# Fused attention and two MLPs: another order of the attention round, casts on ScalarE, and transfers planned by a pipe

## The chip, the cores and the metric

One core of a Trainium2 chip runs the whole program in one launch. The metric is the device time of an execution in microseconds. The kernel before took 1013.02, 1010.97 and 1012.54 us in three runs, median 1012.54. The profiled execution took 1009.88 us.

## The reference

```python
def _attn_ref(q, k, v):                       # q, k, v: 4 x 12 heads x 448 x 64, float32
    S = q.shape[2]
    scores = (1.0 / np.sqrt(q.shape[-1])) * np.matmul(q, k.transpose(0, 1, 3, 2)) - np.log(S)
    return np.matmul(1.0 / (1.0 + np.exp(-scores)), v)
def _moe_ref(x, w_in, w_out):                 # 1792 x 768, 768 x 2048, 2048 x 768; weights float64
    h = x @ w_in
    return np.where(h > 0.0, h, np.exp(np.minimum(h, 0.0)) - 1.0) @ w_out
def _moe2_ref(x, w_in, w_out):
    h = x @ w_in
    return (h - np.tanh(h)) @ w_out
```

The attention output, with its heads side by side, goes through the first MLP and that through the second.

## The kernel before

**Attention.** Two heads make a pair (n = 0 to 23), two pairs a round (m = 0 to 11). A head has 448 keys: three blocks of 128 and a rest of 64. For each pair TensorE transposes q and k (`t`), VectorE or ScalarE copies the result out of PSUM (`plain`), VectorE casts it (`hi`, L335) and takes what the cast lost (`lo`, L339), TensorE makes three blocks of scores (`s`, L358), ScalarE takes their sigmoid (`sig`, L379), and TensorE multiplies by v (`pv`, L387). The keys' rests of both pairs of a round share one product (`sr`, L369), one sigmoid (`sigr`, L375, tile `ar`) and one value product (`pvr`, L397), which closes the sums that `pv` opened. VectorE copies the sums out (`xdone`, L408). Three PSUM buffers go round between `s`, `sr` and every other `t`.

**MLPs.** Each is done by Strassen's seven products with one level of Winograd sums, and each operand is split into a rounded half and a remainder (`head` on ScalarE, `rest` on VectorE), so a product is three matmuls. Tokens are in two halves (s = 0 with 512 columns, s = 1 with 384). T1 to T4 are sums of blocks of attention output (L759), L769 and L775 split them. Products P1, P2, P5, P6, P3, P7, P4 are L803. `snap` (L815) saves a product from PSUM, `h_add` (L820) adds the next.

**Preparation during attention.** Weights come as float64 and are narrowed with integer operations: one step on ScalarE (L598), two on VectorE (L601, L605). All of the first `w_out` (16 loads of 768 KB, L649) is narrowed, summed (L658) and stored again (L663) while attention runs, and four blocks of `w_in` too (L580, L582, tiles R1a, R1b).

**What sets the order.** Nothing is scheduled on the chip: each engine runs its list in order and waits on semaphores. The lists come from a planner (`Sched`). It first places the attention alone by the phases of a round (`PHASES`, in ns), then all of it again; there an operation of the MLPs may take an engine only if the next attention operation of that engine is not put off by more than `GIVE`. All loads and stores are issued by SP's queue (SyncE), in one order too.

Of the kernel before, what the change touches and what calls it, by code (L numbers as in the profile page):

```python
# [9 lines left out]
F32 = mybir.dt.float32  # L10
# [6 lines left out]
class Sched:  # L17
# [3 lines left out]
    def __init__(self):  # L21
        self.ops, self.before, self.plan = {}, {}, {}
# [7 lines left out]

    def emit(self, only_plan=False):
        ops, plan, late = self.ops, self.plan, 0

        planned = {q: sorted((k for k in plan if ops[k][0] == q), key=plan.get, reverse=True) for q in ("ACT", "DVE")}
        after = {k: [a for a in o[3] if a in ops] for k, o in ops.items()}
# [11 lines left out]
        while any(ready.values()):  # L47
            best = None
            for queue, keys in ready.items():
                t0 = free.get(queue, 0)  # L50
                for k, t in keys.items():
                    c = (max(t, t0), ops[k][4], str(k))
                    if k not in plan and planned.get(queue) and c[0] + ops[k][1] > plan[planned[queue][-1]] + late + GIVE:
                        c = (10 ** 9,) + c[1:]
                    if best is None or c < best[0]:
                        best = c, queue, k
            (start, rank, _), queue, k = best
            start = max(ready[queue][k], free.get(queue, 0))
            if k in plan:
                late = start - plan[k]  # L60
# [22 lines left out]
GIVE = 100  # L83

ROUND = 2 * CYCLE
PHASES = {
    "s": ((0, 600, 1200), (3900, 4500, 5100)), "sig": ((1100, 2100, 3100), (5100, 6100, 7100)),
    "pv": ((5900, 6650, 7400), (8150, 8900, 9650)), "pvr": 10500, "xdone": (11400, 12000),
    "sr": -700, "sigr": 50,
    "t": (2000 - ROUND, 2900 - ROUND), "plain": (2950 - ROUND, 4100 - ROUND), "hi": (4100 - ROUND, 5800 - ROUND), "lo": (4700 - ROUND, 6400 - ROUND),  # L90
# [4 lines left out]
SHIFTS = {(0, "ldv"): -12000, (0, "sr"): 2550, (0, "sigr"): 2600, (0, "ldvr"): -11000}  # L95
# [3 lines left out]
def kernel(  # L99
# [67 lines left out]
    with tc.manual_schedule():  # L167
# [7 lines left out]
        def attention():  # L175
# [31 lines left out]
            vrest = [vs_p.tile([128, NR, D], F32, name=f"vrest{i}") for i in range(2)]  # L207
# [20 lines left out]
            def rests(w, g):  # L228
                return heads[w][2 * NR * g:2 * NR * (g + 1), KW:S]

            def ld_kr(g):
                for y in range(NR):
                    i, x = divmod(y, 2)
                    nc.sync.dma_start(
                        out=krest[g % 2][RS * x:RS * x + RS, i].rearrange("p (h d) -> p h d", h=2),
                        in_=rests(0, g)[2 * y:2 * y + 2].rearrange("h p d -> p h d"),
                    )

            def ld_vr(g):
                for z in range(2):  # L240
                    for x in range(2):
                        nc.sync.dma_start(
                            out=vrest[g % 2][RS * z:RS * z + RS].rearrange("p (i x) d -> x p i d", x=2)[x],
                            in_=rests(1, g).rearrange("(i x h) p d -> x h p i d", x=2, h=2)[x, z ^ x],
                        )
# [18 lines left out]
            def when(kind, n, *rest):  # L264
                at = PHASES[kind]
                if kind not in ("sr", "sigr", "pvr", "ldk", "ldv"):
# [6 lines left out]
            def loads(m):  # L273


                g = m * NL // NR
                todo = [("ldv", m, 0, NL)]
                if m * NL % NR == 0:
                    todo = [("ldkr", g)] + todo + [("ldvr", g)]
# [5 lines left out]
                fns = {"ldv": ld_v, "ldkr": ld_kr, "ldvr": ld_vr, "ldkfirst": lambda i: ld_first("k", i), "ldqfirst": lambda i: ld_first("q", i)}  # L285
                for x, key in enumerate(todo):
# [3 lines left out]
                        "ldkr": [("t", NR * (g - 2) + 2)], "ldvr": [("pvr", 2 * (g - 2) + 1)],  # L290
                    }.get(kind, [])
                    sch.op(key, "SP", {"ldkr": 2400, "ldvr": 2400}.get(kind, 600), lambda fn=fns[kind], args=args: fn(*args),
                           after, when("ldv" if kind[2] == "v" else "ldk", m) + x, 2500)

            def loaded(kind, n):
# [4 lines left out]
                return part + ([("ldkr", n // NR)] if n % 2 == 0 else [])  # L300
# [8 lines left out]
            def transpose(n):  # L309
# [5 lines left out]
                for c in range(R):  # L315
                    nc.tensor.transpose(ps[:, DD + KW + c * SP:DD + KW + (c + 1) * SP], ql[:, n % NL, c], ident[:SP, :SP])

            def parts_of(n):
                lo, hi = DD * (n % 2), DD + EW
                return [("ACT", lo, DD + KW), ("DVE", DD + KW, hi)] if n == 0 else [(("DVE", "ACT")[n % 2], lo, hi)]  # L320

            def to_plain(n, x):
# [10 lines left out]

            def hi(n):
                nc.vector.tensor_copy(out=es[n % 2][:, :EW], in_=kq(n))  # L335
# [45 lines left out]
            def pv(n, u):  # L381
                m, x = divmod(n, 2)
                if (x, u) == (0, 0):
                    T["o", m] = pso.tile([128, 2, BK], F32, tag="o", name="pvps")
# [6 lines left out]
            def pv_rest(m):  # L391
                a = T.pop(("a", m))
                for x in range(2):
                    n = 2 * m + x
                    for j in range(2):
                        lanes = slice(64 * (j ^ x), 64 * (j ^ x) + 64)
# [1137 lines left out]
```

## Time and profile before

| | |
|---|---|
| median of three runs | 1012.54 us |
| profiled execution | 1009.88 us, span 1008.2 us |
| PE busy | 977.1 us, 97% |
| DVE, ACT, POOL busy | 780.1, 597.4, 112.1 us |
| granted TensorE clock | 0.988 of full speed, mean |
| HBM traffic | 142.61 MB read, 74.97 MB written |

PE, DVE, ACT and POOL are TensorE, VectorE, ScalarE and GpSimd. Attention takes PE until 171.2 us, the first MLP follows. Since PE is busy nearly everywhere, the places to look at are those where it is not.

### The profile page before, as it was taken

How to read it: one execution, taken by the hardware profiler on the slowest of the kernel's cores; microseconds unless marked ns; L12 is line 12 of the kernel's file. 1: busy time of each engine (PE TensorE's matmuls, PEld its weight loads, DVE VectorE, ACT ScalarE, POOL GpSimd, SP SyncE). 2: the span in 40 equal slices, each digit the busy share in tenths (PEclk: the TensorE clock that was granted, in tenths of full speed). 3: DMA queues.
4: the chain of work that ended last, by engine and by line, in shares of the span. 5: the costliest groups of instructions: out<-in, count | busy, mean ns of one | idle time of the engine just before them, and what ended most of it. 6: DMA issues, size and time to landing. Idle time of an engine off the chain costs nothing.

```text
span 1008.2 us, 15604 instructions
## 1 busy us (share of the span) xinstructions
PE 977.1 (97%) x5306; PEld 844.7 (84%) x5306; DVE 780.1 (77%) x1143; ACT 597.4 (59%) x943; POOL 112.1 (11%) x110
## 2 busy tenths in 40 slices
PE   8989899689999999999999998999999999999998
PEld 5555455578888888888899997888888999999998
DVE  4879798977888888668887899777777788665673
ACT  4768578756666667665566654444444556446652
POOL 2211220202222220000000201111111000000000
PEclk9989899989999999999999999999999999999999
DMA  7899981066666679999984734455555894455442
GB/s 205 286 299 317 300 300 64 31 186 191 191 191 191 191 241 321 372 401 382 373 284 131 242 97 148 160 196 188 186 192 187 325 330 146 125 169 173 128 148 85
DMA packets 145087, 218.61 MB, mean 217 GB/s; under 512 B 21936, under 2 KB 103408, under 8 KB 144752
## 3 DMA queue, kind: packets, MB, share of 16 engines
q1 hardware_dynamic: 143744, 217.10, 64.6%
q8 instruction: 41, 0.67, 0.3%
q10 hardware_dynamic: 1264, 0.52, 0.2%
q14 instruction: 38, 0.31, 0.1%
HBM read 142.61 MB, written 74.97 MB: 216 GB/s over the span
## 4 chain that ended last, share of the span: by engine, by line
PE 90%; DMA 4%; DVE 2%; ACT 1%; issue 1%; SPq 0%; ACTq 0%; DVEq 0%
PE psa L803 13%; PE psd L803 12%; PE psx L803 10%; PE psu L958 7%; PE psv L958 7%; PE psw L958 7%; PE psa L958 6%; PE psb L958 6%; PE psb L803 5%; PE psy L958 5%; PE sps L358 4%; PE pvps L387 4%; PE psx L958 3%; PE psd L958 1%; DMA XB<-in_moe_w_out_dram 1%; DMA vl<-in_v_dram 1%
## 5 line engine op out<-in xcount | busy, mean ns | idle before, releaser
L930 ACT ACTIVATE XB<-t 128x384 fp32r<-128x384 f32 (+1 forms) x111 | 62.0, 562 | 37.5 <-PE psw L958 9.9
L718 POOL TENSOR_TENSOR second<-second 128x384 f32<-128x384 f32 x15 | 19.2, 1279 | 552.1 <-DMA t<-x_forms 213.5
L934 DVE TENSOR_TENSOR XB<-t,XB 128x384 fp32r<-128x384 f32 (+1 forms) x111 | 68.3, 626 | 11.4 <-ACT XB L930 11.1
L379 ACT ACTIVATE an<-sps,bias 128x896 f32<-128x896 f32 x72 | 68.6, 1008 | 3.7 <-PE pvps L387 2.0
L358 PE MATMUL sps<-e 64*128 64x448 f32 x432 | 55.1, 395 | 9.7 <-ACT ar L375 9.3
L358 PEld LDWEIGHTS sps<-e 64*128 64x128 f32 x432 | 40.3, 197 | 25.1 <-ACT ar L375 10.5
L930 ACT ACTIVATE XB<-spare 128x512 fp32r<-128x512 f32 (+1 forms) x72 | 41.1, 573 | 27.0 <-PE psw L958 11.2
L387 PE MATMUL pvps<-an,vl 128*64 128x448 f32 x288 | 56.8, 543 | 0.0
L803 PE MATMUL psa<-XB,W 128*128 128x512 f32 x192 | 54.6, 393 | 0.0
L934 DVE TENSOR_TENSOR XB<-spare,XB 128x512 fp32r<-128x512 f32 (+1 forms) x72 | 44.2, 622 | 8.0 <-ACT XB L930 7.7
L958 PE MATMUL psu<-XB,XB 128*128 128x384 f32 (+1 forms) x192 | 46.3, 348 | 0.0
L226 POOL COPY first<-raw_qk 128x384 f32<-128x384 f32 (+1 forms) x44 | 34.2, 798 | 109.1 <-DMA raw_qk<-in_k_dram 79.5
L958 PE MATMUL psv<-XB,XB 128*128 128x384 f32 (+1 forms) x192 | 46.1, 348 | 0.0
L958 PE MATMUL psw<-XB,XB 128*128 128x384 f32 (+1 forms) x192 | 46.1, 348 | 0.0
L387 PEld LDWEIGHTS pvps<-an,vl 128*64 128x64 f32 x288 | 19.6, 137 | 31.6 <-issue 29.1
L803 PEld LDWEIGHTS psa<-XB,W 128*128 128x128 f32 x192 | 36.4, 190 | 7.7
L832 ACT ACTIVATE spare<-t 128x512 f32<-128x512 f32 (+1 forms) x33 | 19.0, 579 | 36.9 <-DVE t L820 35.9
L718 POOL TENSOR_TENSOR first<-first,second 128x384 f32<-128x384 f32 x30 | 40.1, 1336 | 1.2
L803 PE MATMUL psd<-XB,W 128*128 128x512 f32 x144 | 37.0, 401 | 1.5 <-DVE W L735 1.3
L836 ACT ACTIVATE spare<-spare 128x512 f32<-128x512 f32 (+1 forms) x64 | 36.6, 572 | 0.7
L958 PE MATMUL psa<-XB,XB 128*128 128x384 f32 (+1 forms) x156 | 36.8, 347 | 0.0
L958 PE MATMUL psb<-XB,XB 128*128 128x384 f32 (+1 forms) x156 | 36.8, 347 | 0.0
(362 smaller groups left out, 2732.6 us busy)
## 6 DMA issues: line engine op xcount, KB each, us to landing
x_forms<-R1b SPq DMA_DIRECT2D x58, 256.0 KB, 2.0
first<-p_forms SPq DMA_DIRECT2D x36, 384.0 KB, 6.3
t<-x_forms SPq DMA_DIRECT2D x64, 192.0 KB, 2.9
t<-x_forms SPq DMA_DIRECT2D x47, 256.0 KB, 4.9
x_forms<-t SPq DMA_DIRECT2D x44, 256.0 KB, 2.0
x_forms<-R1b SPq DMA_DIRECT2D x58, 192.0 KB, 4.7
spare<-x_forms SPq DMA_DIRECT2D x36, 256.0 KB, 4.7
x_forms<-t SPq DMA_DIRECT2D x44, 192.0 KB, 3.4
```

The source lines that it names most:

```text
L226: nc.gpsimd.tensor_copy(out=(ql, kl)[w][:, n % NL].rearrange("p c (h d) -> p c h d", h=2), in_=x)
L358: nc.tensor.matmul(out=ps[:, j, :S], lhsT=e[lanes, EW * kz + u * 128:EW * kz + (u + 1) * 128], rhs=e[lanes, EW * qz + KW:EW * qz + EW], st ...
L379: nc.scalar.activation(out=a, in_=T.pop(("s", n, u))[:, :, :S], func=ACTF.Sigmoid, bias=bias, scale=scale)
L387: nc.tensor.matmul(out=T["o", m][D * j:D * j + D, j ^ x, :S], lhsT=vl[m % NVL][:, x, 3 * j + u], rhs=a[:, j], start=(u == 0), stop=False,)
L718: by.tensor_tensor(out=out, in0=x, in1=y, op=op)
L803: nc.tensor.matmul(out=ps, lhsT=w[wz][:, k0:k0 + 128], rhs=xs[xz][:, kk], start=(opens and n == 0), stop=(n == 3 * KH - 1), skip_group_che ...
L832: nc.scalar.activation(out=r, in_=h, func=ACTF.Tanh)
L836: nc.scalar.activation(out=r, in_=r, func=ACTF.Exp, scale=-1.0)
L930: nc.scalar.activation(out=at_place(og_place[i, s, p, j], 0, i)[:, :HW[s]], in_=T["graw", i, s, p, j], func=ACTF.Copy)
L934: nc.vector.tensor_tensor(out=lo, in0=T.pop(("graw", i, s, p, j)), in1=f(hi), op=ALU.subtract)
L958: nc.tensor.matmul(out=T["o2", tag], lhsT=lhsT, rhs=rhs, start=(p in OPENS and j == 0 and x == 0), stop=(j == NG - 1 and x == 2), skip_gro ...
```

## The change

Round: `pvr` now comes ahead of `pv` on TensorE, opens the sums and waits for nothing that `pv` makes; each pair has a PSUM bank of its own, so `xdone` waits for its own pair's `pv` only. The rests lie on other lanes, and the loads of `w_in` need no swapped halves and are one DMA, not three. `hi` of even pairs is on ScalarE. The rests' loads come two DMAs a round instead of four every other round. In the planner a DMA now lands when a pipe shared by all has moved it (`moves`, ns for each kind), `w_out` loads start a round earlier and are paced, an attention operation on ScalarE or VectorE may be put off by 0.6 of its slack, and only TensorE's lateness counts as lateness. The s = 1 operands are made in one piece of 1152 columns, not three of 384, and T3 and T4 of that half are summed on GpSimd. Line numbers after the change are 7 to 27 higher.

```diff
+SLACK = 0.6
+PACE = 7500
-    "s": ((0, 600, 1200), (3900, 4500, 5100)), "sig": ((1100, 2100, 3100), (5100, 6100, 7100)),
-    "pv": ((5900, 6650, 7400), (8150, 8900, 9650)), "pvr": 10500, "xdone": (11400, 12000),
+    "s": ((0, 650, 1250), (3850, 4500, 5100)), "sig": ((700, 1600, 2500), (5200, 6100, 8250)),
+    "pvr": 5800, "pv": ((7400, 8150, 8900), (9650, 10400, 11150)), "xdone": (9750, 12000),
...
+        return {k: plan[k] + SLACK * (t - plan[k]) for k, t in found.items()}
...
-                    if k not in plan and planned.get(queue) and c[0] + ops[k][1] > plan[planned[queue][-1]] + late + GIVE:
+                    if k not in plan and planned.get(queue) and c[0] + ops[k][1] > limit[planned[queue][-1]] + late + GIVE:
...
+            if k in self.moves:
+                moved = max(moved, start + 1400) + self.moves[k]
+                done[k] = moved + 600
...
+            def ld_rests(w, m):
+                g, i = m // 2 % 2, m % 2
+                for x in range(2):
+                    h = 4 * m + 2 * x
+                    to = vrest[g][RS * x:RS * x + RS, i] if w else krest[g][RS * x:RS * x + RS, i].rearrange("p (h d) -> p h d", h=2)
+                    nc.sync.dma_start(out=to, in_=heads[w][h:h + 2, KW:S].rearrange("h p d -> p h d"))
...
+                if hi_on(n) == "ACT":
+                    nc.scalar.activation(out=es[n % 2][:, :EW], in_=kq(n), func=ACTF.Copy)
...
-                        lanes, c = slice(64 * j, 64 * j + 64), 64 * (j ^ x)
+                        lanes, c = slice(64 * j, 64 * j + 64), 64 * x
...
-                        out=T["o", m][D * j:D * j + D, j ^ x, :S], lhsT=vl[m % NVL][:, x, 3 * j + u], rhs=a[:, j], start=(u == 0), stop=False,
+                        out=T["o", m][D * j:D * j + D, x, :S], lhsT=vl[m % NVL][:, x, 3 * j + u], rhs=a[:, j], start=False, stop=(u == 2), skip_group_check=True,
...
-                    op(("pvr", m), "PE", 850, pv_rest, [("sigr", m), ("ldvr", n // NR)] + [("pv", n - y, 2) for y in range(2)])
+                    op(("pvr", m), "PE", 850, pv_rest, [("sigr", m), ("ldvr", m)] + opens)
...
-                        op(("xdone", y), "DVE", 680 if pairs[y][0] == 2 else 630, xdone, [("pvr", m)] + (before if y == 2 * NP else []))
+                        op(("xdone", y), "DVE", 680 if pairs[y][0] == 2 else 630, xdone, [("pv", y, 2)] + (before if y == 2 * NP else []))
...
-                return (slice(None),) if i else range(KH)
+                return (slice(None),) if i or s else range(KH)
...
-                return "DVE"
+                return "POOL" if (i, s) == (0, 1) and x in ("T3", "T4") else "DVE"
...
-                    op("p_load", (j, c), "SP", 600, p_load, [("s", 1, 0)] + (was[c:c + 1] if wide else held), 11000)
+                    sch.moves["p_load", j, c] = 2150
+                    paced = (2 * j + c) * PACE // CYCLE
+                    op("p_load", (j, c), "SP", 600, p_load, ([("s", paced, 0)] if paced else [("t", 1)]) + (was[c:c + 1] if wide else held), 11000)
```

**ScalarE, attention, the fourth and fifth `ar` of the program.** Before, in the round that ends in the first long wait (L598 narrows; R1a is a `w_in` block, XB_71 and XA_70 hold blocks of `w_out`):

```order
L375 ACTIVATE ar<-sps,bias 128x896
L379 ACTIVATE an<-sps,bias 128x896 x3
L327 ACTIVATE plain_122<-sps 128x832
L379 ACTIVATE an<-sps,bias 128x896 x2
L598 ACTIVATE XB_71<-XB_71 128x768
L379 ACTIVATE an<-sps,bias 128x896
L598 ACTIVATE XB_71<-XB_71 128x768
L598 ACTIVATE R1b<-R1a 128x768
L375 ACTIVATE ar<-sps,bias 128x896
```

After, around the narrowing of the same block (L394 is `ar`, L398 `an`, L352 the cast, L605 narrows):

```order
L394 ACTIVATE ar<-sps,bias 128x896
L398 ACTIVATE an<-sps,bias 128x896 x4
L340 ACTIVATE plain_122<-sps 128x832
L352 ACTIVATE e_83<-plain_121 128x832
L398 ACTIVATE an<-sps,bias 128x896
L605 ACTIVATE R1b<-R1a 128x768
L398 ACTIVATE an<-sps,bias 128x896
L394 ACTIVATE ar<-sps,bias 128x896
L398 ACTIVATE an<-sps,bias 128x896
L605 ACTIVATE XB_71<-XB_71 128x768
```

The narrowing has moved from behind the round's last `an` to between two of them.

**SP's queue, the round with most bytes.** Before, from behind one load of `vl` (L259) up to the next, without that first load:

```order
L663 DMA p_forms<-XB_71 128x384
L242 DMA vrest_117<-in_v_dram 64x2x64 x4
L580 DMA R1a<-in_moe_w_in_dram 64x6x256
L582 DMA R1a<-in_moe_w_in_dram 64x3x256 x2
L234 DMA krest_116<-in_k_dram 64x2x64 x4
L663 DMA p_forms<-XB_71 128x2x384
L222 DMA raw_qk<-in_k_dram 128x2x192
L222 DMA raw_qk<-in_q_dram 112x2x256
L222 DMA raw_qk<-in_k_dram 128x2x192
L222 DMA raw_qk<-in_q_dram 112x2x256
L649 DMA XA_70<-in_moe_w_out_dram 128x1536 x2
L663 DMA p_forms<-XB_71 128x4x384
```

After, the fullest round, with its load of `vl` (L274):

```order
L274 DMA vl_119<-in_v_dram 128x4x192
L260 DMA vrest_117<-in_v_dram 64x2x64 x2
L670 DMA p_forms<-XB_71 128x4x384
L656 DMA XB_71<-in_moe_w_out_dram 128x1536
L260 DMA krest_116<-in_k_dram 64x2x64 x2
L249 DMA raw_qk<-in_k_dram 128x2x192
L249 DMA raw_qk<-in_q_dram 112x2x256
L656 DMA XA_70<-in_moe_w_out_dram 128x1536
L249 DMA raw_qk<-in_k_dram 128x2x192
L249 DMA raw_qk<-in_q_dram 112x2x256
L624 DMA kept_wi_2_708<-R1b 128x768
L594 DMA R1a<-in_moe_w_in_dram 128x6x256
```

The big loads now stand apart, and the rests are two DMAs each. A row's bytes are its product times 4.

**VectorE, behind the attention.** Before, from the split of B11 (L775, into R0a) to the sum T3 (the third L759):

```order
L775 TENSOR_TENSOR R0a<-R1a,R0a 128x384 x3
L735 TENSOR_TENSOR R0b<-second,R0a 128x768
L735 TENSOR_TENSOR W_1728<-spare,e_83 128x384
L759 TENSOR_TENSOR R1a<-R1a 128x384 x3
L820 TENSOR_TENSOR t<-t,psb 128x512
L775 TENSOR_TENSOR XB_1805<-R1b,XB_1805 128x384 x3
L820 TENSOR_TENSOR t<-t,psa 128x512
L775 TENSOR_TENSOR R0b<-R1a,R0b 128x384 x3
L759 TENSOR_TENSOR R1a<-R1b,R1a 128x384 x3
L820 TENSOR_TENSOR t<-t,psd 128x512
L846 SCALAR_TENSOR_TENSOR t<-spare,t 128x512
L759 TENSOR_TENSOR R1a<-R1a 128x384 x3
```

After, from the same split (L782) on (L766 is the sum T2, L853 the activation's last step):

```order
L782 TENSOR_TENSOR R0a<-R1a,R0a 128x1152
L782 TENSOR_TENSOR XB_1804<-R1b,XB_1804 128x1152
L742 TENSOR_TENSOR R0b<-second,R0a 128x768
L782 TENSOR_TENSOR R0b<-R1a,R0b 128x1152
L742 TENSOR_TENSOR W_1731<-spare,e_83 128x384
L766 TENSOR_TENSOR R1a<-R1b,R1a 128x3x384
L827 TENSOR_TENSOR t<-t,psb 128x512
L827 TENSOR_TENSOR t<-t,psd 128x512
L827 TENSOR_TENSOR t<-t,psa 128x512
L782 TENSOR_TENSOR XB_1804<-R1a,XB_1804 128x1152
L853 SCALAR_TENSOR_TENSOR t<-spare,t 128x512 x2
L782 TENSOR_TENSOR XB_1804<-R1b,XB_1804 128x1152
```

T1 has gone ahead of the attention's end, T3 and T4 to GpSimd, where they stand behind the last of the attention's copies:

```order
L253 COPY first<-raw_qk 128x384
L253 COPY first<-raw_qk 112x512
L766 TENSOR_TENSOR R1a<-R1a 128x3x384
L766 TENSOR_TENSOR R1b<-R1b,R1a 128x3x384
L725 TENSOR_TENSOR second<-second 128x384
```

GpSimd has nothing else to do in between.

## Rows read from the trace of the kernel before

**Rows 1.** The page: busy time (share of the span) and instructions of each engine.

```profile
PE 977.1 (97%) x5306; PEld 844.7 (84%) x5306; DVE 780.1 (77%) x1143; ACT 597.4 (59%) x943; POOL 112.1 (11%) x110
```

**Rows 2.** Timeline of PE in attention: start, length (us), engine, line, tiles, count, idle.

```profile
61.53 1.49 PE L358 MATMUL sps<-e 64*128 64x448 f32 x12
...
66.90 1.49 PE L358 MATMUL sps<-e 64*128 64x448 f32 x6 [3.89 <-ACT ar L375]
...
111.55 1.49 PE L358 MATMUL sps<-e 64*128 64x448 f32 x6 [4.73 <-ACT ar L375]
...
124.72 0.47 PE L358 MATMUL sps<-e 64*128 64x448 f32 x2
...
160.97 4.76 PE L358 MATMUL sps<-e 64*128 64x448 f32 x36
```

**Rows 3.** Windows: stretch, length, busy us of the engines, granted clock, DMA share, GB/s.

```profile
48.00:60.00 12.00, 12.00 (x95) 6.80 (x94) 11.93 (x15) 9.02 (x10) 4.04 (x6) 1.00 1.05 366
...
61.53:124.72 63.19, 53.84 (x369) 31.31 (x365) 48.46 (x70) 41.09 (x48) 12.69 (x16) 0.89 0.94 302
...
124.72:160.97 36.25, 36.25 (x278) 20.62 (x274) 33.49 (x51) 27.41 (x32) 6.68 (x8) 1.00 0.77 260
...
192.00:204.00 12.00, 3.65 (x18) 3.04 (x18) 12.00 (x25) 8.56 (x18) 0.00 (x0) 0.92 0.17 66
```

**Rows 4.** Waits of PE over the span: total us, times, longest.

```profile
PE sps L358 <- ACT ar L375: 9.3, 3, 4.7
...
PE psd L803 <- ACT R1b L815: 7.2, 1, 7.2
```

**Rows 5.** Timeline of ACT in the two long waits.

```profile
65.06 0.89 ACT L598 ACTIVATE R1b<-R1a 128x768 f32<-128x768 f32 x1 [6.43 <-DMA R1a<-in_moe_w_in_dram]
...
108.68 0.89 ACT L598 ACTIVATE XB<-XA 128x768 f32<-128x768 f32 x1 [1.97 <-DMA XA<-in_moe_w_out_dram]
```

**Rows 6.** DMA issues: form, count, KB each, median us to landing.

```profile
XB<-in_moe_w_out_dram SPq DMA_DIRECT2D x8, 768.0 KB, 8.9
```

**Rows 7.** Timelines behind the attention: PE, DVE and ACT.

```profile
171.23 2.34 PE L803 MATMUL psa<-XA,e 128*128 128x512 f32 x9
...
204.46 1.01 PE L803 MATMUL psd<-XB,R0a 128*128 128x384 f32 x2 [7.21 <-ACT R1b L815]
...
172.44 1.89 DVE L775 TENSOR_TENSOR XB<-R0a,XB 128x512 fp32r<-128x512 f32 x3
...
190.14 2.31 DVE L759 TENSOR_TENSOR R1a<-R1b,R1a 128x384 f32<-128x384 f32 x3
...
203.92 0.49 ACT L815 ACTIVATE R1b<-psd 128x384 f32<-128x384 f32 x1 [2.12 <-DVE R1a L775]
```

**Rows 8.** Groups by shape: line, tiles, shapes, count, busy us, mean ns, idle.

```profile
L327 ACT ACTIVATE plain<-sps 128x832 f32<-128x832 f32 x12 | 10.4, 867 | 6.6 <-PE sps L316 6.6
...
L335 DVE CAST e<-plain 128x832 fp32r<-128x832 f32 x24 | 16.4, 684 | 2.5 <-PE sps L358 1.0 <-ACT plain L327 1.0
...
L775 DVE TENSOR_TENSOR XB<-R0a,XB 128x1536 fp32r<-128x1536 f32 x3 | 5.3, 1756 | 2.0 <-ACT XB L769 2.0
...
L718 POOL TENSOR_TENSOR first<-first,second 128x384 f32<-128x384 f32 x30 | 40.1, 1336 | 1.2
```

**Rows 9.** Timeline of PE, rest products in a clean round.

```profile
159.30 0.98 PE L397 MATMUL pvps<-ar,vrest 64*64 64x448 f32 x8
...
160.11 0.54 PE L369 MATMUL sps<-plain 64*64 64x448 f32 x2
```

**Rows 10.** Timelines of DVE and POOL while POOL adds.

```profile
184.84 1.49 DVE L775 TENSOR_TENSOR XB<-R1b,XB 128x384 fp32r<-128x384 f32 x3
...
186.48 0.69 DVE L820 TENSOR_TENSOR t<-t,psa 128x512 f32<-128x512 f32 x1
...
187.08 3.13 DVE L775 TENSOR_TENSOR R0b<-R1a,R0b 128x384 fp32r<-128x384 f32 x3
...
187.17 1.34 POOL L718 TENSOR_TENSOR first<-first,second 128x384 f32<-128x384 f32 x1
```

More of the change, by code (lines that the diff above doesn't have):

```diff
@@ L21, in __init__ @@
     def __init__(self):
-        self.ops, self.before, self.plan = {}, {}, {}
+        self.ops, self.before, self.plan, self.moves = {}, {}, {}, {}
     def op(self, key, queue, cost, fn, after, rank, latency=60):
@@ L29, in chain, with latest @@
         self.before.update(zip(keys[1:], keys))
+    def latest(self):
+        ops, plan = self.ops, self.plan
+        users, last = {k: [] for k in plan}, {}
+        for k in plan:
+            for a in ops[k][3]:
+                if a in plan:
+                    users[a].append(k)
+        found = {}
+        for k in sorted(plan, key=plan.get, reverse=True):
+            queue, cost, latency = ops[k][0], ops[k][1], ops[k][5]
+            if queue in ("PE", "SP"):
+                found[k] = plan[k]
+            else:
+                by = [found[u] - cost - latency for u in users[k]]
+                if queue in last:
+                    by.append(last[queue] - cost)
+                found[k] = max(plan[k], min(by, default=plan[k]))
+                last[queue] = found[k]
+        return {k: plan[k] + SLACK * (t - plan[k]) for k, t in found.items()}
     def emit(self, only_plan=False):
-        ops, plan, late = self.ops, self.plan, 0
+        ops, plan, late, moved = self.ops, self.plan, 0, 0
         planned = {q: sorted((k for k in plan if ops[k][0] == q), key=plan.get, reverse=True) for q in ("ACT", "DVE")}
+        limit = self.latest() if plan else {}
         after = {k: [a for a in o[3] if a in ops] for k, o in ops.items()}
@@ L59, in emit @@
             if k in plan:
-                late = start - plan[k]
+                late = start - plan[k] if queue == "PE" else late
                 if queue in planned:
@@ L206, in attention @@
             krest = [ld_p.tile([128, 2, DD], F32, name=f"krest{i}") for i in range(2)]
-            vrest = [vs_p.tile([128, NR, D], F32, name=f"vrest{i}") for i in range(2)]
+            vrest = [vs_p.tile([128, NR // 2, 2, D], F32, name=f"vrest{i}") for i in range(2)]
             heads = [x.rearrange("b h s d -> (b h) s d") for x in (k, v)]
@@ L265, in when @@
                 at = PHASES[kind]
-                if kind not in ("sr", "sigr", "pvr", "ldk", "ldv"):
+                if kind not in ("sr", "sigr", "pvr", "ldk", "ldv", "ldqk1"):
                     n, x = divmod(n, 2)
@@ L332, in kq, with hi_on @@
                 return plain[n % 2][:, DD * (1 - n % 2):][:, :EW]
+            def hi_on(n):
+                return "DVE" if n == 0 or n % 2 else "ACT"
             def hi(n):
-                nc.vector.tensor_copy(out=es[n % 2][:, :EW], in_=kq(n))
+                if hi_on(n) == "ACT":
+                    nc.scalar.activation(out=es[n % 2][:, :EW], in_=kq(n), func=ACTF.Copy)
+                else:
+                    nc.vector.tensor_copy(out=es[n % 2][:, :EW], in_=kq(n))
             def lo(n):
@@ L573, in load @@
                     nc.sync.dma_start(out=t[:, :CW], in_=kept[key])
-                elif key[:2] == ("wi", 0):
-                    f0 = key[2] * 128
-                    to = (t.bitcast(I32) if wide else t[:, :CW]).rearrange("p (k f) -> p k f", k=KD)
-                    rows = w_ins[0][:, f0:f0 + 128].bitcast(dt)
-                    nc.sync.dma_start(out=to[:64], in_=rows.rearrange("(k z p) f -> z p k f", z=2, p=64)[0])
-                    for x in range(2):
-                        nc.sync.dma_start(
-                            out=to[64:].rearrange("p (m x) f -> x p m f", x=2)[x],
-                            in_=rows.rearrange("(m x z p) f -> x z p m f", x=2, z=2, p=64)[1 - x, 1],
-                        )
                 elif wide:
@@ L1099, in job @@
                     after.append(("keep", kept_by[key], key))
+                if place == 4:
+                    sch.moves["load", n] = 2700
                 raw_op(("load", n), "SP", 600, lambda: load(n, key, not live), after, 8500 if place == 4 else 8500 if live else 6000)
@@ L1115, in job @@
                     kept_by[key] = n
+                    if place == 4:
+                        fixed["keep", n, key] = n * ROUND + 3
+                    if place == 4:
+                        sch.moves["keep", n, key] = 1100
                     raw_op(("keep", n, key), "SP", 600, lambda: keep(n, key), [done], 12000 if place == 4 else 5600)
@@ L1497, in mlp @@
                 sch.op(k, o[0], o[1], o[2], o[3], fixed.get(k, 10 ** 6 + late_by[k]), o[4])
-            sch.chain([("pvr", NPR // 2 - 1)] + sequence)
+            sch.chain([("pv", NPR - 1, 2)] + sequence)
         attention()
```

75 lines of the change are left out of this document (29 added, 46 removed).

## Prediction

> **What bounds the kernel now.** I read the page first, for how much can be won at all. PE is busy for 977.1 of the 1008.2 us of the span [rows 1], so 31.1 us are idle, and a change that leaves the matmuls alone can win these and what a slow clock adds to them. Then PE's timeline in attention, for where. A round opens with the scores of its even pair. In the clean stretch three rounds take from 124.72 to 160.97, which is 12.08 us each; the four rounds from 61.53 to 124.72 take 63.19 us where four clean ones take 48.33 [rows 2]. So **14.9 us are lost in four rounds of attention**. The windows over the same stretches say what kind of loss it is: PE idles for 9.35 us and has a clock of 0.89 on the mean, where the clean stretch has no idle time and 1.00 [rows 3]. A matmul behind each long wait runs at the lower of the two clocks: 6 of L358 take the 1.49 us that 12 take elsewhere [rows 2]. Nearly all the idle time is one line of the waits, PE's L358 for ACT's `ar` [rows 4], 3.89 and 4.73 us in the two long ones and 0.7 in a third; a long one so costs (14.9 - 0.7) / 2 = 7.1 us with its clock.
>
> ACT is not slow there. It stands in front of a narrowing, L598, whose load has not landed: 6.43 us for R1a at 65.06, 1.97 more for XA at 108.68 [rows 5], and `ar` is queued behind it. The load is late because the DMA engines are full: share 1.05 at 366 GB/s from 48 to 60 us [rows 3]. At that rate a round of 12.08 us moves 4318 KB. Counting SP's order between loads of `vl` (the big ones have 768 KB and land after 8.9 us [rows 6]), the rounds from 51 us on ask for 5120, 4480, 4352, 4480 and 4352 KB, 22784 in all, for which five rounds have room for 21590. No order on ACT could hide that.
>
> The other place lies behind attention. The first product of the MLP starts at 171.23, and before P3 of the second half, at 204.46, PE waits 7.21 us for a snapshot on ACT, which waits for VectorE's last split of T4 [rows 4, 7]. VectorE is busy for all 12.00 us of 192 to 204 [rows 3]. That is the only wait of this size outside attention.
>
> **The change part by part.**
>
> Transfers. After the change the same count gives 4224, 4800, 2688, 4608 and 3840 KB for the five fullest rounds in a row, 20160 in all, under the 21590: the first `w_out` blocks are loaded a round earlier, and the pairs of 768 KB are spread. Two rounds are still over 4318, by 482 and 290 KB, 1.3 and 0.8 us at 366 GB/s. Both are followed by a round with room. So the two long waits go, and I charge 2.1 us for the two overfull rounds as if nothing covered them. Bounds: 0, since 48 to 60 us has a full pipe and no idle PE [rows 3], and 14.9, all of it back. I take 2.1, nearest to the clean row. Term: -14.9 + 2.1.
>
> Casts. Eleven casts leave VectorE (0.68 us each [rows 8]) and go to ACT, which copies as many columns in 0.87 [rows 8]. In attention neither engine sets the end: in the clean stretch ACT is busy for 27.41 of 36.25 us and VectorE for 33.49 [rows 3], and with three casts moved it is 30.0 and 31.4. In the four slow rounds the same preparation fitted into 48.33 us would make ACT 41.09 + 3.5 = 44.6 and VectorE 48.46 - 2.7 = 45.8, 92 and 95%; the order starts it about a round earlier, so some of that moves forward. Cost 0; if the cover is gone (VectorE over 12.08 us in a round) PE waits for the split of q and k, a few tenths a round. What is late next in attention is PE itself.
>
> The rest products. The number of matmuls is the same. The four of `pvr` use the same four quarters of the array in another order; now they take 0.81 us from 159.30 on and the four of `sr` 0.86 to 160.97 [rows 2, 9], so all four overlap, two quarters that share rows and two that share columns among them. Cost 0. If neighbours in the new order did not overlap, both would double, 1.7 us a round and 20 us in all; `sr` already writes two column halves to one bank at once, which speaks against it, and a gain has nothing to come from, since the array is as full. SP's queue: a `w_in` block takes one issue, not three, and a round two plus two rest DMAs instead of runs of eight every other round; its stalls shorten, which is in the term above.
>
> Behind attention. I count VectorE's operations from the first product on (E = 171.23), because PE's wait ends with the last of them. Now it starts its splits at E + 1.2 (172.44), three of 512 columns in 1.89 us, starts the sum T2 at E + 18.9 (190.14), and P3 of the second half starts at E + 33.2 [rows 7]. After: 0.6 for one `xdone` (two took the 1.2), 8 splits of 512 at 0.63 = 5.0, three of 1152 at 1.32 (1.756 us for 1536 [rows 8]) = 4.0, the weights' 768 and 384 = 1.3, T2 itself 1.3: T2 ends at E + 12.2 and no longer at E + 21.2. T1 and two weight sums have gone forward into attention, and one wide instruction has one start-up instead of three.
>
> Then T3 and T4 on GpSimd, 3 x 1.34 = 4.0 us each [rows 8]. Here the trace speaks against the change: while POOL added, three splits of VectorE took 3.13 us instead of 1.49, though an addition of a PSUM operand took its usual 0.69 [rows 10]. Two of the three were held until a GpSimd instruction was over. What follows T2 on VectorE is mostly of the kind that was held: the splits of T2, B22, T3, T4 (1.3 each), three last steps of the activation (0.63 each), one sum (0.6), one weight split (0.9), 8.6 us. T3 holds it to E + 16.2, T4 for 4.0 more, so the last split ends at E + 28.8, the snapshot takes 0.5 [rows 7], and P3 starts at E + 29.3. Gain 33.2 - 29.3 = 3.9 us. Without the holding VectorE is through at E + 12.2 + 1.9 (three additions of products) + 8.6 = E + 22.7, P3 starts at E + 23.2, and the gain is 10.0. I take 3.9, since the held rows are of this very pair of engines. The idle time before P3 is about as long as now, so its slow clock stays.
>
> The Trainium skill states this as a rule, in "SBUF — State Buffer", section "Who interferes with whom": a VectorE instruction with two SBUF inputs and a GpSimd instruction that reads SBUF take one shared port by an exclusive lock for the whole instruction. The trace agrees for instructions of 384 columns; that a 1152-wide one holds VectorE for all of its 4.0 us no run here shows. By the rule the gain is 3.9 us, by a mere sharing of the port nearer to 10.0.
>
> Everything from the second weight group on stays as it is; there PE is busy nearly throughout, and the `w_in` blocks land far ahead.
>
> **Sum** against the profiled execution: 1009.88 - 14.9 + 2.1 - 3.9 = 993.2 us. The median of the runs is 2.66 above that execution, so the time to expect is 995.8.
>
> **The rivals.**
>
> No holding: GpSimd and VectorE share, and nothing is late in the two overfull rounds. 1012.54 - 14.9 - 10.0 = 987.6. For it: in rows 10 every second VectorE instruction still slips in. Against it: the three that took twice as long.
>
> One long wait stays. The narrowings now stand between two sigmoids, close behind their loads, and one load that is late by more than planned repeats the picture of 65.06: 1012.54 - 14.9 + 7.1 - 3.9 = 1000.8, 1003 with the overfull rounds. For it: the two rounds over 4318 KB; against it: the five rounds ask for 1430 KB less than the pipe moves in them, where they now ask for 1194 more.
>
> The waits are only moved: all the same bytes have to go through in attention, and the earlier start changes nothing. Then only the 3.9 us remain: 1008.6. Against it: the clean stretch has a DMA share of 0.77, so there is room to move into.
>
> Slower: ACT's new order makes lateness dear. Before, a narrowing stood behind the round's last `an`, and PE lost 3.89 of ACT's 6.43 us, 2.5 being covered [rows 2, 5]. Now three sigmoids come behind it, and a round's last value product needs them. If loads come over 2.5 us late in several rounds, each costs 7.1 us; from three on (21.3 against the 18.8 won) the kernel is slower, and with four it takes 1022. For it: twenty narrowings are placed this tightly; against it: the bytes a round.
>
> **How the numbers follow.** Forecast 0.47, no holding 0.16, one wait stays 0.20, only moved 0.07, slower by ACT's order 0.10. The range from 985 to 1009 leaves out most of the last case and a little below the second. About 0.2%, 2 us, is what a measurement can tell from no change. Faster by more: the first three and a part of the fourth, 0.85; within it 0.05; slower 0.10.
>
> **What would show it.** Right: round starts 12.1 us apart throughout, PE's wait for `ar` under 2 us in total, a clock of 1.00 until the first product, which starts near 158; full DMA windows with no idle PE; then VectorE splits that take 2 to 4 us beside T3 and T4, and a wait of PE of 6 to 7 us, P3 about 29 us behind the first product. Wrong: PE waiting for `an` or a value product waiting behind a narrowing (the slower rival), rounds over 12.3 us with no wait (rest products that no longer overlap, or VectorE over its round), or a P3 at 23 us.

## The result, and the profile after

The changed kernel takes 998.54 us (median of 4 runs, 998.21 to 999.5) against 1011.75 for the kernel before: ratio 0.9871, 95% interval 0.9854 to 0.9888. On another chip it took 1000.17 against 1008.18, ratio 0.9914 (0.9901 to 0.9927). So it is faster by 0.9 to 1.3%; the forecast of 995.8 was 2.7 us low. Its profiled execution took 998.61 us, with a span of 996.9. The page's busy times, to be read against [rows 1]:

```profile
PE 968.8 (97%) x5306; PEld 837.6 (84%) x5306; DVE 766.8 (77%) x1108; ACT 603.3 (61%) x940; POOL 113.8 (11%) x112
```

The span is 11.3 us shorter, and three places make it up: the first product of the MLP comes 5.66 us sooner, the stretch from there to the second half's P3 is 3.81 us shorter, and the rest 1.8. Those two products in the changed kernel, to be read against [rows 7]:

```profile
165.57 2.34 PE L810 MATMUL psa<-XA,e 128*128 128x512 f32 x9
...
194.99 1.01 PE L810 MATMUL psd<-XB,R0a 128*128 128x384 f32 x2 [7.35 <-ACT R1b L822]
```

PE's waits in attention (us in total, times, longest) answer to [rows 4]:

```profile
PE pvps L404 <- DVE R0a L426: 4.4, 4, 2.0
PE pvps L404 <- DVE R1a L426: 1.8, 2, 0.9
PE pvps L404 <- DVE R1b L426: 1.7, 2, 0.9
PE pvps L404 <- DVE R0b L426: 1.6, 2, 0.8
```

No wait for `ar` is left. In its place stands one that the prediction did not have: a value product (L404) waits for VectorE's copy of the attention output (`xdone`, L426), ten times, 9.5 us. PE's timeline, first a round with that wait and then the start and the end of one without it, to be read against [rows 2]:

```profile
64.48 2.09 PE L377 MATMUL sps<-e 64*128 64x448 f32 x18
...
70.21 0.98 PE L415 MATMUL pvps<-ar,vrest 64*64 64x448 f32 x8
...
71.88 3.23 PE L404 MATMUL pvps<-an,vl 128*64 128x448 f32 x16
75.92 1.72 PE L404 MATMUL pvps<-an,vl 128*64 128x448 f32 x8 [0.82 <-DVE R0a L426]
77.58 0.67 PE L377 MATMUL sps<-e 64*128 64x448 f32 x4
...
130.22 2.08 PE L377 MATMUL sps<-e 64*128 64x448 f32 x18
...
142.26 2.09 PE L377 MATMUL sps<-e 64*128 64x448 f32 x18
```

A round with the wait takes 77.58 - 64.48 = 13.10 us, one without it 142.26 - 130.22 = 12.04. The difference of 1.06 is the wait's 0.82 and some 0.2 more, because the 24 value products take 3.23 + 1.72 us in two parts and 4.73 in one (experiment 1 shows that row). VectorE's side of the same moment shows that it isn't late:

```profile
73.08 0.96 DVE L612 SCALAR_TENSOR_TENSOR XB<-XB 128x768 int32<-128x768 int32 x1
75.15 0.62 DVE L426 COPY R0a<-pvps 128x448 f32<-128x448 f32 x1 [1.11 <-PE pvps L404]
```

VectorE stood idle for 1.11 us until the sixteenth product was through (71.88 + 3.23 = 75.11). That product belongs to the odd pair; the copy reads the even pair's bank, whose last product was the twelfth. So `xdone` does not wait for its own pair's `pv` only, as the description of the change has it.

Behind attention, GpSimd's timeline and VectorE's, to be read against [rows 7, 10]:

```profile
177.68 2.70 POOL L766 TENSOR_TENSOR R1a<-R1a 128x1152 f32<-128x1152 f32 x1 [41.87 <-DVE R1a L766]
180.34 3.79 POOL L766 TENSOR_TENSOR R1b<-R1b,R1a 128x1152 f32<-128x1152 f32 x1
184.09 1.47 POOL L725 TENSOR_TENSOR second<-second 128x384 f32<-128x384 f32 x1
...
189.13 1.99 POOL L725 TENSOR_TENSOR first<-first,second 128x384 f32<-128x384 f32 x1
```

```profile
176.17 1.36 DVE L766 TENSOR_TENSOR R1a<-R1b,R1a 128x1152 f32<-128x1152 f32 x1
...
179.24 2.36 DVE L782 TENSOR_TENSOR XB<-R1a,XB 128x1152 fp32r<-128x1152 f32 x1
181.75 4.36 DVE L853 SCALAR_TENSOR_TENSOR t<-spare,t 128x512 f32<-128x512 f32 x2 [0.15 <-ACT spare L843]
186.03 2.17 DVE L782 TENSOR_TENSOR XB<-R1b,XB 128x1152 fp32r<-128x1152 f32 x1
...
193.07 1.35 DVE L782 TENSOR_TENSOR R1a<-R1b,R1a 128x1152 fp32r<-128x1152 f32 x1
```

A split of 1152 columns takes 1.35 us once GpSimd is done (193.07), 2.36 and 2.17 beside it. P3 follows 29.42 us behind the first product.

### The profile page after: what moved, and what is told of

Its sections match the earlier page's. It is cut to its first block, busy times and chain, and to the rows that moved or that the text cites. A ratio compares the mean times of both kernels' runs of the same rounds, so it can differ in the third digit from the quotient of the medians.

```text
span 996.9 us, 15482 instructions
## 1 busy us (share of the span) xinstructions
PE 968.8 (97%) x5306; PEld 837.6 (84%) x5306; DVE 766.8 (77%) x1108; ACT 603.3 (61%) x940; POOL 113.8 (11%) x112
## 4 chain that ended last, share of the span: by engine, by line
PE 93%; DVE 3%; DMA 1%; issue 1%; ACT 1%; SPq 1%; POOL 0%; POOLq 0%; DVEq 0%; ACTq 0%
PE psa L810 12%; PE psd L810 11%; PE psx L810 10%; PE psu L965 7%; PE psv L965 7%; PE psw L965 7%; PE psa L965 6%; PE psb L965 6%; PE pvps L404 6%; PE psb L810 5%; PE psy L965 5%; PE sps L377 5%; PE psx L965 3%; PE psd L965 1%; PE pvps L415 1%
## 5 line engine op out<-in xcount | busy, mean ns | idle before, releaser
L398 ACT ACTIVATE an<-sps,bias 128x896 f32<-128x896 f32 x72 | 69.7, 1010 | 27.8 <-PE sps L377 27.5
L941 DVE TENSOR_TENSOR XB<-t,XB 128x384 fp32r<-128x384 f32 (+1 forms) x111 | 68.3, 625 | 10.6 <-ACT XB L937 10.5
L404 PE MATMUL pvps<-an,vl 128*64 128x448 f32 x288 | 59.0, 546 | 9.5 <-DVE R0a L426 4.4
L404 PEld LDWEIGHTS pvps<-an,vl 128*64 128x64 f32 x288 | 19.4, 136 | 48.3 <-issue 32.1
L937 ACT ACTIVATE XB<-spare 128x512 fp32r<-128x512 f32 (+1 forms) x72 | 41.3, 574 | 29.7 <-PE psw L965 11.6
L377 PE MATMUL sps<-e 64*128 64x448 f32 x432 | 51.1, 375 | 1.1 <-DVE e L354 0.5
L253 POOL COPY first<-raw_qk 128x384 f32<-128x384 f32 (+1 forms) x44 | 27.8, 657 | 106.6 <-PE sps L325 90.6
```

The source lines that it names most:

```text
L253: nc.gpsimd.tensor_copy(out=(ql, kl)[w][:, n % NL].rearrange("p c (h d) -> p c h d", h=2), in_=x)
L377: nc.tensor.matmul(out=ps[:, j, :S], lhsT=e[lanes, EW * kz + u * 128:EW * kz + (u + 1) * 128], rhs=e[lanes, EW * qz + KW:EW * qz + EW], st ...
L398: nc.scalar.activation(out=a, in_=T.pop(("s", n, u))[:, :, :S], func=ACTF.Sigmoid, bias=bias, scale=scale)
L404: nc.tensor.matmul(out=T["o", m][D * j:D * j + D, x, :S], lhsT=vl[m % NVL][:, x, 3 * j + u], rhs=a[:, j], start=False, stop=(u == 2), skip ...
L937: nc.scalar.activation(out=at_place(og_place[i, s, p, j], 0, i)[:, :HW[s]], in_=T["graw", i, s, p, j], func=ACTF.Copy)
L941: nc.vector.tensor_tensor(out=lo, in0=T.pop(("graw", i, s, p, j)), in1=f(hi), op=ALU.subtract)
```

## The experiments

All are timed against the kernel before on their own chip, and a ratio below is always to that kernel. Experiments on different chips can be compared by these ratios only roughly: the unedited changed kernel gave 0.9871 on one chip and 0.9914 on another, and the two intervals don't touch. Differences under some 4 us between chips are therefore not settled by the ratios; there the text goes by the profiled runs, stretch by stretch.

**1. The copies behind the last value product** (e1_copy_late), for the new wait.

```
- op(("xdone", y), "DVE", ..., xdone, [("pv", y, 2)] + ...
+ op(("xdone", y), "DVE", ..., xdone, [("pv", n, 2)] + ...
```

> The even pair's copy out of the two banks is emitted behind the odd pair's last value product instead of behind its first one; nothing else is edited. Theory A (the copy waits for whatever was written to the two banks as one tile before it, and the next value product waits for the copy, though it writes the other bank): the ten waits of pvps L404 on DVE L426, 9.5 us in the trace of the changed kernel, go; attention's rounds stand 12.0 to 12.2 us apart instead of 13.1; 989 to 990.5 us. Rival B (TensorE waits there because VectorE is truly late, or because the rest products stand ahead): the wait comes back in another place, at the next round's transposes or rest product, and the time is 996 to 1000 us.

990.81 us, ratio 0.9820 (0.9803 to 0.9836), and no wait of L404 is left. PE's timeline of a round, and the windows (length, then busy time of PE, PEld, DVE, ACT, POOL, then clock, DMA share, GB/s) of two rounds:

```profile
61.12 2.09 PE L377 MATMUL sps<-e 64*128 64x448 f32 x18
...
66.85 0.98 PE L415 MATMUL pvps<-ar,vrest 64*64 64x448 f32 x8
...
68.51 4.73 PE L404 MATMUL pvps<-an,vl 128*64 128x448 f32 x24
73.17 0.68 PE L377 MATMUL sps<-e 64*128 64x448 f32 x4
```

```profile
61.12:73.17 12.05, 12.05 (x93) 6.87 (x91) 11.37 (x15) 10.99 (x14) 2.65 (x4) 1.00 1.06 364
85.23:97.28 12.05, 12.05 (x93) 6.88 (x92) 8.49 (x12) 10.71 (x13) 3.04 (x4) 1.00 1.06 369
```

The 24 value products run through and the rounds take 12.05 us. Theory A holds for the wait and the rounds (the time is 0.3 us above its range): the first product stands at 155.69, 9.9 us sooner than in the changed kernel. That the order is kept for the shared tile as a whole is read from the two waits, the copy's and the product's; a tile for each bank was not run. Some is given back: P3 is 9.0 us sooner and the span 6.9 us shorter; 1.8 of the 2.1 us between go behind 606.92 us, where PE runs at a lower clock (see the last section).

**2. T3 and T4 back on VectorE** (e2_sums_on_vector), for the holding.

```
- return "POOL" if (i, s) == (0, 1) and x in ("T3", "T4") else "DVE"
+ return "DVE"
```

> T3 and T4 of the first layer's second half are taken on VectorE, still as one instruction of 1152 each, so GpSimd runs none of them. Theory A (the two GpSimd sums hold VectorE while they run, the estimate behind 'P3 some 29 us behind the first product'): the second half's P3 starts 26 us or less behind the first product behind attention instead of 29.4, 995 to 996 us. Rival B (GpSimd takes work off VectorE, whose stretch there is the longer one): VectorE has 2.4 us more to do before P3, which starts 30 to 32 us behind the first product, 999 to 1001 us.

997.64 us, ratio 0.9892 (0.9876 to 0.9907), between the two forecasts. P3 starts 26.99 us behind the first product, not 29.42, although VectorE does two sums more: the GpSimd sums cost more than they saved. But the end doesn't follow: the span is 996.8 us, and 996.9 in the changed kernel. PE's waits behind attention:

```profile
PE psd L810 <- DVE t L827: 2.3, 1, 2.3
PE psx L810 <- ACT t L822: 2.3, 1, 2.3
PE psa L810 <- DVE t L827: 1.7, 1, 1.7
```

The one wait of 7.35 us has become three, two of them ahead of P3. The wait of 2.3 for `t` comes at 197.01, behind P3's first products, with a lower clock after it (0.83 from 195 to 205 us). It is for a snapshot on ACT, which itself waits 1.41 us for VectorE's L872 ahead of it: VectorE still owes work there that it had put off.

**3. Both together, and GpSimd idle** (e3_late_vector, e8_gpsimd_idle; the second adds the line below), beside an unedited run of the changed kernel on that chip (e0_after, 1000.17 us as above).

```
- return "DVE" if step == (0, 0) else "POOL"
+ return "DVE" if step in ((0, 0), (0, 1)) else "POOL"
```

> The changed kernel once more, unedited, so that the others are compared on one chip: 996 to 999 us.

> Both edits together: the even pair's copy behind the odd pair's last value product, and T3 and T4 on VectorE. Theory A (what T3 and T4 on VectorE gave up to P3, 2.4 us, was lost again to waits of the products behind it, with VectorE the engine that ends last there): as the late copy alone, within 1 us. Rival B (the two gains add): 2 to 2.5 us less than with the late copy alone.

> As with both edits together, and the four sums of the second weight group (L725) on VectorE too, so that GpSimd runs nothing beside VectorE's 1152-wide instructions behind attention. Theory A (VectorE is held while GpSimd runs any such sum, 0.8 us in each of T2's and the others' 2.15 us instead of 1.35): no L766 or L782 of 1152 over 1.4 us there, P3 1.5 to 3 us sooner behind the first product than with both edits alone. Rival B (they are long for another reason, such as ScalarE reading the same buffers): they stay near 2.1 us and P3 comes no sooner. Either way the end of the kernel may not follow, since the products behind P3 wait for VectorE.

988.31 us, ratio 0.9797 (0.9783 to 0.9812), and 986.71 us, 0.9783 (0.9770 to 0.9796). The second is the best version found and beats both kernels. GpSimd and VectorE with both edits:

```profile
167.68 2.12 POOL L725 TENSOR_TENSOR second<-second 128x384 f32<-128x384 f32 x1 [40.02 <-DVE R1a L766]
169.75 2.12 POOL L725 TENSOR_TENSOR first<-first,second 128x384 f32<-128x384 f32 x1
171.84 1.02 POOL L725 TENSOR_TENSOR second<-second,first 128x384 f32<-128x384 f32 x1
```

```profile
167.57 1.35 DVE L782 TENSOR_TENSOR XB<-R1b,XB 128x1152 fp32r<-128x1152 f32 x1
168.84 2.17 DVE L766 TENSOR_TENSOR R1a<-R1a 128x1152 f32<-128x1152 f32 x1
170.93 0.67 DVE L827 TENSOR_TENSOR t<-t,psa 128x512 f32<-128x512 f32 x1
...
172.13 4.03 DVE L782 TENSOR_TENSOR XB<-R1a,XB 128x1152 fp32r<-128x1152 f32 x2
```

VectorE with GpSimd idle:

```profile
168.63 1.35 DVE L782 TENSOR_TENSOR XB<-R1b,XB 128x1152 fp32r<-128x1152 f32 x1
169.91 1.35 DVE L766 TENSOR_TENSOR R1a<-R1a 128x1152 f32<-128x1152 f32 x1
...
172.37 2.62 DVE L782 TENSOR_TENSOR XB<-R1a,XB 128x1152 fp32r<-128x1152 f32 x2
```

P3 of that run, behind its first product:

```profile
155.70 2.33 PE L810 MATMUL psa<-XA,e 128*128 128x512 f32 x9
...
180.63 0.62 PE L810 MATMUL psd<-XB,R0a 128*128 128x384 f32 x2 [0.31 <-ACT R1b L822]
```

The sum T3 (the L766 at 168.84 and 169.91) takes 2.17 us beside GpSimd and 1.35 without it, the two splits behind it 4.03 and 2.62, and P3 moves from 28.04 to 24.93 us behind the first product. The holding is shown, and it makes 2.2 of these 3.1 us; the rest lies in ACT's order, where another operation (L739) stands ahead of the snapshot in the first of the two runs and behind it in the second. Attention took 1.1 us longer with GpSimd idle, and a wait of 2.6 us comes behind P3's first products, so the span is only 1.2 us shorter; the medians differ by 1.6, within the intervals. For the two edits together, the median lies 2.5 us under the late copy's, as rival B had it, but on another chip and with overlapping intervals, so that isn't settled.

**4. Without the pipe model, and without the pacing** (e4_no_pipe on the changed kernel; e10_no_pipe and e12_unpaced on the best version, where no round has a wait that could hide something).

```
- if k in self.moves:
+ if k in ():                       # e4, e10
- ([("s", paced, 0)] if paced else [("t", 1)]) ... fixed[k] = 2 * k[1] * PACE
+ [("s", 1, 0)] ... fixed[k] = (2 * k[1] + 2) * CYCLE    # e12
```

> The scheduler no longer moves a transfer's planned end behind the transfers before it (the two lines that add to 'moved' do nothing); the new due times and the loads paced 7.5 us apart stay. Theory A (the spacing of loads by due times is what ended the long waits of attention): no wait on a load over 1 us, 998 to 1000 us. Rival B (the pipe model does it): waits of TensorE for ACT's sigmoid behind a narrowing that waits for its load come back, in sum 3 to 15 us, 1001 to 1013 us.

> As the kernel with the late copy and GpSimd idle behind attention (986.7 us), without the pipe model (the two lines do nothing). Theory A (the pacing by due times is enough; the 0.8 us waits covered nothing): within 1.5 us of it. Rival B (in the changed kernel those waits hid loads that came late): waits of ScalarE's narrowings on loads, and of TensorE behind them, 2 to 8 us more.

> As the kernel with the late copy and GpSimd idle behind attention (986.7 us), with the weights' loads due every 6 us again and only behind the second pair's first scores, as before the change; the pipe model stays. Theory A (the pacing is what keeps a round's bytes under what a round can move): long waits of ScalarE's narrowings on loads come back, 4 to 14 us more. Rival B (rest loads round by round and the early rest products leave room for it): within 1.5 us.

1001.43 us, ratio 0.9927 (0.9912 to 0.9943); 987.91, 0.9795 (0.9782 to 0.9808); 987.74, 0.9793 (0.9778 to 0.9808). The first lies in rival B's range, but not by rival B's mechanism: ACT waits 0.5 us in all for loads there, and PE never for `ar`. Its first product is 1.7 us later, with twelve waits of some 0.8 us for a copy instead of ten. On the best version neither part, left out alone, costs more than can be measured at the end; leaving out both at once was not run. Without the pipe model the rounds stay at 12.05 us and the first product stands at 154.86; P3 then follows after 29.7 us, not 24.9, with a wait of 2.8 us for ACT's half of a weight (L739) on the way, and yet the span is only 1.0 us longer. Without the pacing the first product does not stay. First product and P3 of the unpaced kernel:

```profile
162.28 2.34 PE L810 MATMUL psa<-XA,e 128*128 128x512 f32 x9
...
184.31 0.62 PE L810 MATMUL psd<-XB,R0a 128*128 128x384 f32 x2 [1.11 <-ACT R1b L822]
```

Attention takes 6.6 us longer (155.70 in the best version), with short waits of the transposes for q and k (2.6 us in seven) and a lower clock behind them (0.88 from 130 to 142 us); but P3 follows after 22.0 us, not 24.9, and the span is 1.6 us longer in all. VectorE had done in attention what it would have done behind it: the sum T1 and five of the eight splits of 512 columns.

**5. The transfers alone** (e5_before_pipe): the kernel before with `moves`, `latest`, the due times, the pacing and the rule that only TensorE's lateness counts, and nothing else of the change.

> The kernel before with the transfers' part of the change alone: the pipe model, the due times, the loads paced 7.5 us apart, the limit by the latest start. Rest products behind the value products, rest loads four pairs at a time, casts and sums as before. Theory A (the 14.9 us that four rounds lost came from transfers alone): no wait of TensorE over 2 us in attention, rounds 12.0 to 12.2 us apart, 11 to 15 us less than before. Rival B (the rest loads of four pairs still overfill two rounds, so that it takes both parts): 3 to 8 us of waits stay, 4 to 10 us less than before.

1002.59 us, ratio 0.9939 (0.9921 to 0.9958): 5 to 6 us less than before, in rival B's range. Waits of PE, then of ACT from 20 to 160 us:

```profile
PE sps L386 <- ACT ar L403: 6.1, 3, 3.3
```

```profile
ACT R1b L627 <- DMA R1a<-in_moe_w_in_dram: 13.9, 4, 5.5
ACT XB L627 <- DMA XB<-in_moe_w_out_dram: 9.2, 3, 5.0
```

Narrowings still wait for loads, and `ar` behind them. In the changed kernel ACT waits 1.7 and 0.3 us on the same two. So spreading the weights' loads alone does not end the waits; the longest is 3.3 us, where it was 4.7.

The bytes of a round don't tell these kernels apart either. Counted as in the prediction, five rounds in a row ask for at most 20672 KB here, under the 21590 that was taken as the room, and 6.1 us of waits for `ar` stay. The unpaced kernel of experiment 4 asks for 22656 KB in five rounds, nearly the 22784 of the kernel before, and has no wait for `ar` at all.

**6. The rest products behind again** (e13_rest_behind, on the best version): the dependences of before for `pvr`, `sr`, `xdone` and all the phases of before (those of `plain` and `hi` too), with rest loads round by round and the casts on ACT.

```
- "pvr": 5800, "pv": ((7400, 8150, 8900), (9650, 10400, 11150))
+ "pv": ((5900, 6650, 7400), (8150, 8900, 9650)), "pvr": 10500
```

> As the kernel with the late copy and GpSimd idle behind attention (986.7 us), but with the rest products back behind the value products, and the phases of before with them; rest loads stay round by round, transfers spread. Theory A (the transfers alone, with the rest loads in every round, end the long waits; the order of the rest products costs and gives nothing): rounds 12.0 to 12.2 us apart, no wait of TensorE over 1.5 us, 985.5 to 988.5 us. Rival B (a rest product that stands last has its sigmoid wait behind ScalarE's narrowings, so that the order does give something): waits of TensorE's next scores on ScalarE's ar as in the kernel before, 4 to 10 us in sum, 990 to 997 us.

994.73 us, ratio 0.9863 (0.9848 to 0.9878), 8 us more. That is in rival B's range, but not for rival B's reason. The wait in attention, and ACT's timeline at one of the eleven:

```profile
PE sps L377 <- ACT plain L340: 8.5, 11, 0.8
```

```profile
68.83 0.90 ACT L352 ACTIVATE e<-plain 128x832 fp32r<-128x832 f32 x1
69.64 0.84 ACT L340 ACTIVATE plain<-sps 128x832 f32<-128x832 f32 x1
```

With the phases of before, the even pair's cast stands ahead of the odd pair's copy on ACT and puts it off by 0.8 us, and the scores wait for that copy. ACT's narrowings wait 12.3 us for loads, and PE waits for `ar` once, 0.2 us; but the rounds take some 13.1 us, which leaves room to cover such waits. So this run doesn't tell which of the two, the rest loads in every round or the early rest products, ended the waits for `ar`.

**7. Casts and pieces** (e6_casts_on_vector on the changed kernel, e9_three_pieces on the best version).

```
- return "DVE" if n == 0 or n % 2 else "ACT"
+ return "DVE"                                              # e6
- return (slice(None),) if i or s else range(KH)
+ return (slice(None),) if i else range(KH)                 # e9
```

> The even pair's cast goes back to VectorE (0.6 us a round more there, 0.8 to 0.9 us a round less on ScalarE); all else as in the changed kernel. Theory A (the cast is hidden on either engine): the same, 997.5 to 999.5 us. Rival B (VectorE, which makes the scores' operands in time only with that cast gone, now ends last): 12 rounds with 0.3 to 0.6 us more wait each, 1002 to 1006 us.

> As the kernel with the late copy and GpSimd idle behind attention (986.7 us), with the second half's sums, heads and rests in three pieces of 384 again. From the kernel before, three pieces of a rest took 1.89 us where one of 1152 takes 1.35, and three of a sum 1.49 against 1.35: about 3 us more on VectorE before P3, which starts 2 to 4 us later behind the first product. Theory A: the end follows by 1 to 3 us, as VectorE ends last there. Rival B (products behind P3 wait for VectorE's later work all the same): the end moves by under 1 us.

1000.38 us, ratio 0.9916 (0.9900 to 0.9932), with the first product at 165.92: the time lies between the two forecasts, and the span (997.0 against 996.9 us) and the first product (165.92 against 165.57) say that the cast costs nothing that shows on either engine. 988.81 us, 0.9801 (0.9787 to 0.9815): P3 starts 28.27 us behind the first product, not 24.93, so the wide instructions are worth 3.3 us there; the span grows by 0.4 and the median by 2.1, undecided between the two theories.

## Why the prediction was right, and where not

The time lay in the range and the side was right: the long waits in attention went, and the stretch behind it shrank. The size was partly luck. By the prediction's own sum the profiled execution should have taken 993.2 us; it took 998.61, 5.4 more, and the median missed by 2.7 only because it lies 0.07 us below the profiled run, where 2.66 above was added. By the number alone the rival with one long wait (1000.8) was a little nearer than the forecast; the waits rule it out, since none for `ar` is left. Term by term:

- **Transfers**, -14.9 + 2.1. The -14.9 came. The 2.1 for overfull rounds were nothing: a round at a DMA share of 1.06 runs in 12.05 us without a wait (experiment 1). The reason was only half right. Bytes per round were said to decide; but the waits for `ar` stay in a kernel that asks for fewer bytes than the room (5) and are gone in one that asks for more (4). In the latter attention takes 6.6 us longer, with short waits for q and k, and the whole program 1.6. What ends the waits for `ar` is something that experiment 5 lacks: the rest loads in every round, the early rest products, the `w_in` block as one DMA (13.9 us of ACT's waits in 5 are for such blocks, still loaded by three) or the moved casts. Which, stays open.
- **Rest products, "Cost 0"**: the step that failed. The overlap that it argued is there: from the first rest product to the first value product 70.21 to 71.88 is 1.67 us, as before [rows 2, 9]. But the step looked at the array alone. With the rest products first, the copies may follow each pair's last value product instead of the pair's joint end, and the even pair's copy is then emitted between the odd pair's products. Both pairs share one two-bank tile, so the copy waits for the odd pair's product written before it, and the next product waits for the copy. That is 10 times 1.06 = 10.6 us, estimated from the one round; experiment 1 got 9.9 us back with nothing changed but when the copy is emitted. "Rounds over 12.3 us with no wait" was the sign named for a failure here; the rounds came, at 13.1, with a wait.
- **The first product** so came at 165.57, not near 158: 9.9 more for the copies, 2.1 less for overfull rounds that cost nothing, and 0.6 less elsewhere.
- **Casts**, 0: right (7), if they stand where the change puts them; ahead of the copy they cost 8.5 us of waits (6).
- **Behind attention**, -3.9, P3 at E + 29.3: it measured -3.81 and E + 29.42, by errors that cancelled. T3 and T4 took 2.70 and 3.79 us where 4.0 each was taken, but GpSimd went straight on to the second weight group's four sums, to 191.12, and held VectorE there too, which the prediction left out. The holding itself is as predicted. The split at 179.24 ends at 181.60, 1.26 us behind T4's start at 180.34, where T3 is through, and T4 ends at 184.13, 2.53 us behind the split: each takes about its own time once the other is through (1.35 us for a split alone, 2.70 for T3, which ran mostly beside additions of PSUM operands). This is what the Trainium skill, "SBUF — State Buffer", section "Who interferes with whom", states for a whole instruction, and these rows show it at 1152 columns. Without any holding P3 came at E + 24.93 (3), with the two sums, 2.7 us, on VectorE itself; less these it would be 22.2, an estimate, where the prediction had 23.2.
- **Everything from the second weight group on**: 1.8 us came from there unasked. PE has the same three waits there in both kernels (1.0, 0.6 and 1.3 us); the last ends at 625.05 before and at 615.64 after. PE's windows behind it, before and then after:

```profile
625.00:630.00 5.00, 4.95 (x15) 3.93 (x16) 2.98 (x5) 1.12 (x2) 0.00 (x0) 0.66 0.80 241
```

```profile
615.00:620.00 5.00, 4.36 (x19) 3.64 (x20) 3.68 (x6) 1.52 (x3) 0.00 (x0) 1.00 0.78 230
620.00:625.00 5.00, 5.00 (x26) 4.38 (x25) 2.58 (x4) 1.37 (x3) 0.00 (x0) 1.00 0.79 269
```

From that wait's end to the end of the program it is 1.9 us less, and up to it nothing is won.

Of the rivals, the one without holding is answered by the splits of 2.36 and 2.17 us, and the one with waits only moved by the -14.9 that came. The slower one had no footing: ACT waits 2.0 us in all for the weights' loads in attention, and no wait of PE there is put down to a narrowing (in the second trace of the same kernel, e0_after, one of 0.8 us is, one of the ten).

## What to carry to other kernels

When work is reordered, follow each release as well as each cost: a copy that may start earlier is emitted earlier, and if it shares a tile with products still to be written, it waits for them and they for it, at a gap in the dense engine every round. A gain on one stretch reaches the end only as far as the second engine is not behind there: VectorE's debt turned 2.4 us into nothing and 6.6 into 1.6, so measure a stretch by the engine whose work was put off. Work given to GpSimd beside VectorE has to be priced with what it holds up, to the last instruction that GpSimd runs there, and not only to the ones that were moved.

## What the runs showed of the hardware

Ten waits, at most one in a round, nine of 0.82 to 0.89 us and one of 1.96, left PE's granted clock at 1.00, its level of 2.4 GHz, throughout attention in the changed kernel, so that one of 0.82 us cost only 1.06; the waits of 3.9 and 4.7 us before, with a lower clock behind them, cost some 7 each [rows 2, 3]. And the clock can differ with the same waits: PE idles for the same 1.0, 0.6 and 1.3 us from 611 to 625 us before and from 601 to 616 after, yet the 5 us that follow run at 0.66 in one, between its two levels, and at 1.00 in the other; with the late copy, whose wait ends at 606.92, they run at 0.66 again. Such a term of 1.9 us comes and goes between kernels whose programs are alike there; why was not found. A GpSimd sum of 384 columns took 1.02 us where it began while VectorE was adding a PSUM operand (171.84), and 2.12 beside VectorE's instructions with two SBUF operands (experiment 3).
